# GpSimd makes every second low part of the MLP's hidden tiles, with new orders of the same matmuls and an earlier form of the last division

## The chip, the core and the metric

The kernel runs on one core of one Trainium2 chip. A core has five engines each with its own stream of instructions, which this kernel writes out by hand: TensorE (PE in the profile; PEld is its loading of weights), VectorE (DVE), ScalarE (ACT), GpSimd (POOL) and SyncE (SP), which here issues most of the transfers. They wait for one another through semaphores. Matmuls write to PSUM, of which the kernel uses eight banks of 128 partitions by 512 numbers in 32 bits; VectorE and ScalarE read the results there.

The metric is device time in microseconds, the median of three runs; less is better. Before the change it is 1000.59 us (1000.38 to 1000.65).

## The reference

An input x of 2048 rows by 448 columns is normalized, and two branches of the result are added to x: attention of 16 heads, 28 wide, that share one key and one value head, and a dense layer with ReLU, 1792 wide.

```python
xn = _layernorm(x, axis=-1)
return x + _A_ref(xn, A_wq, A_wk, A_wv, A_wo) + _B_ref(xn, B_w1, B_w2)

# _A_ref
scores = jnp.einsum("bhqd,bkd->bhqk", q, k) * (Dh ** -0.5)
p = _softmax(scores, axis=-1)
o = jnp.einsum("bhqk,bkd->bhqd", p, v)
... o @ wo
# _B_ref
h = jnp.maximum(jnp.einsum("bsd,df->bsf", x, w1), 0)
return jnp.einsum("bsf,fd->bsd", h, w2)
```

## The kernel before

**Precision.** Most products are made from a high part H in the format fp32r and a low part L, the rest: three passes, H by H, H by L and L by H, stand for one product. So every operand needs two instructions after it leaves PSUM: ScalarE copies the high part, and VectorE subtracts it from the bank to get the low part.

**The head** (to about 62 us). Rows are taken in four blocks of 512, four x tiles each. x arrives in `acc`, wq, wk and wv in `stg`. For each block the statistics are taken (L330, L331), x is normalized, transposed on TensorE (L371) and copied to `xt` in two parts (L373, L374). Four projections follow (`qkv_proj`, L429; L438 for the first three of block 0), each written out by `qkv_out`: ScalarE's and VectorE's `qs` (L415, L416), then a store to `qscr` in DRAM. Keys and values ride along in the spare columns of the four groups; `k_rows` (L400) picks the keys out of the `qs` of groups 0 and 1 with four matmuls, and `k_diff` makes differences of keys on GpSimd (`kD`, L411).

**The transfers' slots.** The transfers of SyncE and ScalarE share eight semaphores in turn, so an issue waits until the transfer eight places before it has landed.

**The MLP** (62 to about 384 us) has 28 tasks, seven parts of the weights by four blocks. A task has two up tiles (128 hidden columns by 512 rows: L707 `b<-xt,w`) and, two tasks later, four down tiles (128 rows by 448: L707 `b<-w,hH` and `b<-w,hL`). Each matmul uses 32 of the 128 rows of the array, and four row groups, numbered 0 to 3, work side by side. When an up tile is done, ScalarE makes hH with ReLU (L722) and VectorE hL (L724). When a down tile is done, ScalarE copies it to `y` (L731) and GpSimd adds that to `acc` (L732). GpSimd also splits the weights of the next part, in six steps over the tiles of one task in four (L306, L308).

**The maxima.** Softmax needs for each query the largest score. For each of 16 units (a block by a group of four heads) 64 matmuls of the high parts (L567) give scores whose maximum VectorE takes (L571): a single maximum. Or a pair: one matmul gives scores a, a second, with `kD`, gives the differences d, ScalarE makes max(d, 0) (`more`, L764), and VectorE adds it to a and takes the maximum (L575, with a short second instruction for the result): two maxima for one VectorE job. 445 of the 1024 maxima are made during the MLP.

**The attention** (384 to about 986 us). Scores (L609, three matmuls each), their exponentials on ScalarE (L620), p @ v (L827, four matmuls for one tile of 128 keys, 256 groups in all) and the output projection (L867). The sums of exponentials come with p @ v as a row of their own. The first 15 units are divided by way of DRAM; the last in `finish`: before the change a matmul with `dsel` spreads each sum over its head's rows, VectorE takes reciprocals of 128 columns (L894), GpSimd multiplies, and the last output projection (L904), its sum and its stores follow, the last tile in two halves on two queues.

**The order** is written out in two tables. In `ROWS` (MLP) a digit lets a row group issue its next matmul; a to d begin a tile, e to h join one, i to l make a single maximum, m to p and q to t the two halves of a pair, A to D early scores, each with the bank behind it; v takes a VectorE job that is owed. In `ORDER` (attention) `V` is a number of p @ v groups, `B` a burst (scores, maxima ahead by row group, maxima behind, banks), `O` and `f` matmuls of the output projection. The engines keep that order.

Of the kernel before, what the change touches and what calls it, by code (L numbers as in the profile page):

```python
# [8 lines left out]
F32 = mybir.dt.float32  # L9
# [22 lines left out]
    a3b4c5012012012012012d60123012301230123013o7i23f5s13e41g33vA0123012012p001vA2t2012012012p1012t7012vA  # L32
    0f6i21h51g431m0vA231q723123vA1a12310231023vA10231023f302l710g6l2102l01vA02h41023102vA31e52310231vA02
    310231023f10k7310k2310k0h3vA10310310vA31c7e6312031vB20312031203vAn2203r020h12vA0j43203203j5vA03e73vB
    03c3032b0302vB1302120d412vA031g1301230j5vA230f33201h02i21vA321i6321e432vA103f7203102l5vA01c2h30123e0
    123vB02310231023vA10g4l6102l512e3h21vA203b12031203vAg001320132i6h712i5312e231vA2031c303120vA31203102
    3f4i6213i0213e12vA1d502130213vA0f22301k63103vA10h3k01031g503vAj72032b40321vA3a621302130g11vA03120f53
    201p22e41t0201l7201h6201320f3vB32013e52130vAk0130g4l7102h11vA02310231i22vA312a031g602310vA23j5023020
    3j7vA2e33b20h41g003vA12302130213vA021302l510c71l1021vAh002130213i42vAf63i52132e213vB210d121031203vAf
    00313013vA0o41h70s31301c63f1023120132i5123vAa312301g230j02vA03f6203102l41vAe12l510210h321vA032f70321  # L40
    03vA21e63k00310l4g1102h21vA023102312i5vA312a031g303120vA32j40230j1230vA2j5e730h6g030vAf32301230123vA
    0123012d410c1vA3j5023f00231023vA1i6231m2231q3231vBa5230230vA2h003k60f430vAk331e1c7310231vA02h5102312
    03vA12301k2301k630h71k00vA31c3032f50321vA3e4213201h121vA031o203f7s60130k0130g5130213vB20132f303210vA
    321e7k6l0101g40l2102vAf102d51023e31vA23012301320vA13201l6201l0a7210g5vA1h32013203b22vA0321032103vAc6
    10d0210321302vA1320312e53o410l1s310h60g71302f0vA30123e212301vA23102l3102l1f502l41vA02101201g0vAl3012
    f6h7021vA230123i11231vAi5g231i423e023vA0b323012301vA230120l112e61vA20d5f7023103g3vA103210321i4321m0h
    2212q13vA1g53i6213e3213021vB302b4302130k1vA130c61e53201vA20h312031203vA120312i03132i7vA1d12f53213vAe
    4k213013c31302vA1h620j0230vA2f1302130k7130vA1k5301c23012vA30f3231i0213e12vA1h40210k73103vAf60k53103e
    31vA3k00130g11302vA103210231e2vA21l7021h30g43012vA30j523023e6j02vA30j12h20b72310vA32103210321vA031c5
    0d3b02031vA2031201321e732103vA2f2032103102vA310231e0k110d4j6g730vA230f323012301vA23e512l201g0l1012l6  # L50
    0vA12h702130213vA02130g413203vAj220h0b1203123vAe312301o6310s7310k2h5f4031013g1vB01230123012vA30j7232
    0b23k01e4vA31k60310g3h1102vA31023f5023i71vA23e212301l020vA1d62013021vA0321e13k4103c71032vB01320b0320
    13vA2i41321h221a3vB23103f620312vA031g003210p421e7t1210l52102h310g23vB123012301230vA23j102h0j50g630vA
    f33201321i432vA13i221h7i1213vA2e03j5203023vA02b4301g33012vA3e6123120312vA0j22d10k030f73g40vA13203120
    321vA0l52102d31g1031vA2i2312e431203vB12032103k0b50vA3c20132e11320vB1l620120h41203vA1g3031i03213vAe22
    3102l7012vA0f1l620120h51vA2i4132i013213vAf2c73123e312vA31023120312vA0n63k40r10h2f7k0vA031301g53012vB
    31023102d4i1vA32j032e7f3302vA130213021l20vA21p60g41t121vAe52h7102310231023vA1c003j22032f4d102130vB21
    302130c61vA30123e0j7203b220312vB0132013201l3vA2e41l702f1h0021vA30g213021302vA13e623102l5102l31c70l42
    10vA2h210231023vAf002310k53103g1vA10h7213i3213vAe22j4302f6302vA3102l510201d0vA2e731023103k31vA03o410
    3s210vA1e110g0d5f720312301vA230123012301o3h60b4s2301g5301230213e0213021302vA130o7130s2103vAc31e52012  # L60
    0f0021vAh40120312i1132vAi2132f5a73210vA32103c6103210vA23102f33i021p121t2vAg7e41l50212h601230vB123012
    301o03vA013s20h71k50303f6c1vB310231e323120vAl21201l520f7g40vA1l0201h12013vA210321032b20vA3120312e612
    0l5120h310k73f1vA0c0130213e212vB3012301203j5vA203b62031e123vA102l7102h201c4301vB230123e01230vA21302d
    510k7310g23j1203f4vA230123012h60vA12310g53102vA3n323r72i13f02e43120vBc23102301203120vAl712e5l11201g6
    0vAh4120310321vA032e2j33203j720h0f52vA03120132013vAa12130k4130k3f2301c7vA30120312e631vA201p520f1t421
    02h2103vA120312031203b3k00310h11vAc430123e71230vA213021302p210t51k001g1h4vA0213023023b6vB2302301g3l5
    vAi0121h72e41vA3201320n2302r1vA032j5032e632j00vB320f43c101320vA1h320123i5123vA1i223f7g6312vA31i02312
    e13120vA3120c4031vA20l5120h612e331vA2031203f1k2301c03012h40vB1321032103vA2j5032b203210h1vA213i6213e4
    2310vB3c7103201h0201vA23012i5312a6310k33vAf40k1310g2310vA2310123e71230vAj52h60b33021302vA130213e0213
    021h70o13j50s43f603g31032vA103210h221203vA1203f7o4031s513i1g613e3213021vB302f03021032vA10o51l7s11e2h  # L70
    3k4013vAk6013013013c1vB013201d720vA23b42031203vA10c33123e1123vA01230213021vA03o510l0s61h31g73vAf123i
    2132e4132vA013210p6210t0vA2f30210l5210h112301vBk2301c030f7230vA123e312l5021vAh402103k6103k11vA03c21e
    0320132vA012301230j5vA2303n3e7r60vAh2k1f003g41031230vB123013201p5vA20j1t620f220h012vA30123a313201vA3
    0c6130b12012vAl5012e2120vA12l70120h31203vA120312a03103c4vA03210h62j5023n2023r7vAe123f3031g0013vB2013
    201321023f4023vA10k5l710g31h0201vA320132e6j2320vAj5230g130h42vA0j73203f02031vA203123102vAd31023103j2
    2e43j5203f6c70vA3210l0201h120vA123e312301k20vA31031o5031s4vA031e7301c030f3230120d21vA20312a413201vA3
    20f7302130213012vA3i51g33i6123f4e02vA102l1120h712vA031g2031203j5vA230j6230b32h40vA13201321032vA1i132
    1m53f02q7vA1l6e31g40120vB120p1210t7210vA2d61e23103g310321032vAj50320n72h00r42vA30g6b1321032103210321
    vAa52310k43f2031k7031vAg10h312031203vA1230123012vA30k41d7013e113k0vA0f630g513021vB03210321a33120vA3n
    4203r020h1023j2023e6f723013vBk00130g31h502vA130213a221302vA103201k1301k4301c03vA2i6f33213e721vAh2201  # L80
    32013k11vA03k4f503130vA1h3k603103g21vA03210321032vA1h0i12132i413g7vAa613203f220312vA0p31201t1201vA2e
    0d41203f60231023vA10o5310s131a231k30f03vA01301g63012vBd101230123f42vA032103c710321l3021h6i5231e12vA3
# [85 lines left out]
def attention_plus_mlp(ctx: ExitStack, tc: tile.TileContext, x, wq, wk, wv, wo, w1, w2, out):  # L168
    nc = tc.nc
# [31 lines left out]
    for t in range(TPB):  # L201
        (nc.scalar if t % 2 else nc.sync).dma_start(acc[:, t, :], xv[:, t, :])
# [778 lines left out]
```

## Time and profile before

| | |
|---|---|
| median of three runs | 1000.59 us |
| the profiled execution | 1000.64 us |
| its span, first to last instruction | 998.9 us |
| matmuls (records in the trace) | 11686 |
| granted clock of TensorE, mean | 0.998 |
| transfers: moved, mean rate | 44.04 MB, 44 GB/s |

The profile is of one execution of the kernel. Its page gives the busy time of each engine, the same in 40 slices of the span (digits are tenths), the chain of work that ended last, and the costliest groups of instructions by line, with the mean time of one and the idle time before them with what ended it ("<-"). Further views list windows of time, waits, and the instructions in order of time. A busy TensorE is not one at its peak: its ends are modelled, so matmuls per microsecond say more. A wait counts only where the waiting engine holds up the end.

### The profile page before, as it was taken

Reading aid. Unit: us, or ns where it says so; the run is one execution under the profiler, and the core shown is the slowest. Engines: PE = TensorE matmul, PEld = TensorE weight load, DVE = VectorE, ACT = ScalarE, POOL = GpSimd, SP = SyncE. Lnnn points to the kernel's source line nnn. Section 1 sums busy time; section 2 is a strip of 40 time slices with the busy share of each in tenths; the row PEclk is TensorE's granted clock in tenths of the full one; section 3 lists DMA queues with packets and bytes.
Section 4 is the critical chain, followed back from the end, with each engine's and each line's share of the span. In section 5 each row is a group of like instructions: output and inputs, shape, how many; then the busy total and the mean of one; then the engine's idle time right before and its main releaser. Section 6 shows DMA issues by size and latency. Waiting matters only on the chain.

```text
span 998.9 us, 28752 instructions
## 1 busy us (share of the span) xinstructions
PE 990.0 (99%) x11686; PEld 632.0 (63%) x11686; DVE 716.8 (72%) x1301; ACT 696.2 (70%) x1340; POOL 250.4 (25%) x257
## 2 busy tenths in 40 slices
PE   9999999999999999999999999999999999999998
PEld 8779999999999995444444445444445433446444
DVE  7648999898888898988888876788776543743103
ACT  5533333434344446888899987899998799997993
POOL 4243475564646436010110110110110110110110
PEclk9999999999999999999999999999999999999999
DMA  7742201101010001101011001010111010000001
GB/s 241 259 138 84 62 23 33 42 14 42 14 52 3 14 2 46 33 14 46 13 34 43 26 23 57 16 46 23 24 35 42 31 34 24 13 13 29 23 13 37
DMA packets 31224, 44.04 MB, mean 44 GB/s; under 512 B 12228, under 2 KB 22788, under 8 KB 31092
## 3 DMA queue, kind: packets, MB, share of 16 engines
q1 hardware_dynamic: 24056, 32.72, 10.5%
q10 hardware_dynamic: 7036, 9.49, 3.1%
q8 instruction: 91, 1.49, 0.6%
q14 instruction: 41, 0.34, 0.1%
HBM read 29.62 MB, written 12.44 MB: 42 GB/s over the span
## 4 chain that ended last, share of the span: by engine, by line
PE 98%; DVE 1%; DMA 0%; ACT 0%; issue 0%; POOL 0%; DVEq 0%; ACTq 0%; POOLq 0%
PE o L827 25%; PE b L609 25%; PE b L707 24%; PE b L567 9%; PE b L867 4%; PE o L707 4%; PE b L429 3%; PE b L229 1%; PE b L438 1%; PE b L371 1%; PE o L567 0%; PE b L400 0%; DMA qscr<-qs 0%; PE b L904 0%; DVE rb L894 0%; PE o L429 0%
## 5 line engine op out<-in xcount | busy, mean ns | idle before, releaser
L571 DVE TENSOR_REDUCE nmx<-b 128x1 f32<-128x512 f32 x862 | 551.7, 684 | 158.6 <-PE b L567 110.6
L620 ACT ACTIVATE w<-b 128x512 f32<-128x512 f32 x1023 | 525.5, 616 | 74.1 <-PE b L609 69.5
L609 PE MATMUL b<-q,kHL 28*128 28x512 f32 (+1 forms) x3069 | 333.4, 425 | 0.2
L567 PE MATMUL b<-kHL,qhi 28*128 28x512 f32 x917 | 329.0, 448 | 1.1 <-ACT more L764 1.1
L609 PEld LDWEIGHTS b<-q,kHL 28*128 28x128 f32 (+1 forms) x3069 | 192.8, 183 | 186.3 <-DVE nmx L571 94.4
L707 PE MATMUL b<-xt,w 32*128 32x512 f32 x1974 | 290.7, 393 | 0.0
L707 PE MATMUL b<-w,hH 32*128 32x448 f32 x1616 | 276.0, 368 | 0.0
L827 PE MATMUL o<-w,vtile 128*32 128x512 f32 x2048 | 269.1, 607 | 0.2 <-ACT more L764 0.2
L707 PEld LDWEIGHTS b<-xt,w 32*128 32x128 f32 x1974 | 235.4, 183 | 3.3 <-DVE nmx L575 0.4
L707 PE MATMUL b<-w,hL 32*128 32x448 f32 x808 | 215.0, 364 | 0.0
L707 PEld LDWEIGHTS b<-w,hH 32*128 32x128 f32 x1616 | 206.6, 183 | 3.7 <-ACT y L731 0.5
L567 PEld LDWEIGHTS b<-kHL,qhi 28*128 28x128 f32 x917 | 150.5, 182 | 58.8 <-DVE nmx L571 25.6
L732 POOL TENSOR_TENSOR acc<-y,acc 128x448 f32<-128x448 f32 x112 | 128.0, 1154 | 125.6 <-ACT y L731 125.2
L851 POOL TENSOR_TENSOR on<-rb,oS 128x512 f32<-128x512 f32 x15 | 19.2, 1282 | 516.9 <-DMA rb<-rscr 314.1
L707 PEld LDWEIGHTS b<-w,hL 32*128 32x128 f32 x808 | 126.3, 183 | 0.2
L731 ACT ACTIVATE y<-b 128x448 f32<-128x448 f32 x101 | 54.7, 545 | 97.8 <-PE b L707 79.2
L827 PEld LDWEIGHTS o<-w,vtile 128*32 128x32 f32 x2048 | 43.2, 108 | 83.6 <-issue 78.9
L707 PE MATMUL o<-xt,w 32*128 32x512 f32 x378 | 95.2, 393 | 0.0
L707 PEld LDWEIGHTS o<-xt,w 32*128 32x128 f32 x378 | 66.9, 183 | 0.6 <-SPq L711 0.3
L764 ACT ACTIVATE more<-b 128x512 f32<-128x512 f32 x52 | 31.0, 598 | 38.8 <-PE b L567 27.8
L707 PE MATMUL o<-w,hH 32*128 32x448 f32 x176 | 50.5, 365 | 0.0
L722 ACT ACTIVATE hH<-b 128x512 fp32r<-128x512 f32 x47 | 28.0, 598 | 31.5 <-PE b L707 27.5
(112 smaller groups left out, 733.3 us busy)
## 6 DMA issues: line engine op xcount, KB each, us to landing
qscr<-qs SPq DMA_DIRECT2D x16, 512.0 KB
q<-qscr SPq DMA_DIRECT2D x12, 512.0 KB
rb<-rscr SPq DMA_DIRECT2D x60, 64.0 KB
out<-acc SPq DMA_DIRECT2D x15, 224.0 KB
acc<-in_A_x SPq DMA_DIRECT2D x14, 224.0 KB
qhi<-qscr SPq DMA_DIRECT2D x11, 256.0 KB
stg<-in_B_w ACTq DMA_DIRECT2D x5, 448.0 KB
q<-qscr ACTq DMA_DIRECT2D x4, 512.0 KB
```

The costliest lines, as they stand in the source:

```text
L429: nc.tensor.matmul(pq, w, xm, start=n == 0, stop=n == len(steps) - 1)
L567: nc.tensor.matmul(pm, qhi[u][rows, s * P : (s + 1) * P], k.rearrange("p k b q -> p (k b q)"), start=True, stop=True)
L571: nc.vector.tensor_reduce(dst, pm, axis=AX.X, op=ALU.max)
L609: nc.tensor.matmul(ps, keys, qst[u][rows, s, :], start=k == 0, stop=k == 2)
L620: nc.scalar.activation(p, ps, AF.Exp, scale=SCALE)
L707: mm = nc.tensor.matmul(o, w, m, start=self.left == self.n_mm - 1, stop=self.left == 0)
L722: nc.scalar.activation(hH, self.ps, AF.Relu)
L731: nc.scalar.activation(y, self.ps[:, 0:D], AF.Copy)
L732: nc.gpsimd.tensor_tensor(a, y, a, op=ALU.add)
L764: nc.scalar.activation(more, d[1], AF.Relu)
L827: nc.tensor.matmul(o_acc[u][RB * j : RB * (j + 1)], vtile[:, kb, :], ps[j], start=kb == 0, stop=kb == NKB - 1)
L867: nc.tensor.matmul(py[:, 0:D], om[:, i * P : (i + 1) * P], wm, start=n == 0, stop=n == len(steps) - 1)
```

## The change

It does six things.

- **Loads of the head.** Each of the first four x tiles comes in two halves of 224 columns, one from SyncE and one from ScalarE.
- **Key rows.** In blocks 1 and 2 `k_rows` and `k_diff` come after the fourth projection instead of before it; blocks 0 and 3 keep their place.
- **Low parts.** For the second up tile of each task ScalarE copies the ReLU twice, as hH and as `h` in full precision, and GpSimd subtracts. The buffers of `y` go from four to three.
- **ROWS** is a new table: 344 singles and 54 pairs instead of 319 and 63, with single maxima first; 443 VectorE jobs become 432.
- **ORDER** is a new table: 572 maxima instead of 579, 246 bursts instead of 247, the same scores and p @ v.
- **finish**: TensorE transposes the last unit, VectorE takes the four reciprocals of each row, GpSimd spreads them, TensorE transposes that back, VectorE multiplies; the last tile is summed and stored whole.

```diff
 ROWS = """
-    a3b4c5012012012012012d60123012301230123013o7i23f5s13e41g33vA0123012012p001vA2t2012012012p1012t7012vA
+    a3b4c5012012012012012d60123012301230123013k7i13f53g3e413vA2013201l22vA01l0201201l7vA201201201l1vA201
...
 ORDER = """
-    V2 R B6.0111..1265043162 B6.0.01.540316245 B4.11.001.063512641 B0.001..063 V2 B4.12.0.5421063 V1
+    V2 R B6.111.0.3204561235 B6.11.1.064312650 B0.0..1 V1 B7.000.113.4302165431062 V1 B4.02.1.1546320 V1
...
     for t in range(TPB):
-        (nc.scalar if t % 2 else nc.sync).dma_start(acc[:, t, :], xv[:, t, :])
+        for queue, cols in ((nc.sync, slice(0, D // 2)), (nc.scalar, slice(D // 2, D))):
+            queue.dma_start(acc[:, t, cols], xv[:, t, cols])
...
         qkv_out(b, 2, qkv_proj(b, 2))
-        k_rows(b, qs)
-        k_diff(b)
+        if last:
+            k_rows(b, qs)
+            k_diff(b)
...
         pq = qkv_proj(b, 3, middle=None if last else lambda: transposed(b + 1, xn))
         qkv_out(b, 3, pq)
+        if not last:
+            k_rows(b, qs)
+            k_diff(b)
...
                 nc.scalar.activation(hH, self.ps, AF.Relu)
+                if self.i == 1:
+                    h = dpool.tile([P, QB], F32, name="h")
+                    nc.scalar.activation(h, self.ps, AF.Relu)
+                    nc.gpsimd.tensor_tensor(hL, h, hH.bitcast(F32), op=ALU.subtract)
+                    return
                 owed.append(
...
-            y = dpool.tile([P, D], F32, name="y", bufs=4)
+            y = dpool.tile([P, D], F32, name="y", bufs=3)
...
-        for _ in range(3):
+        pt = [bank(i) for i in range(TPB)]
+        for _ in range(2):
             next(piece)
         for i, c in enumerate(cols):
-            pb = bank(i)
-            nc.tensor.matmul(pb[:, 0:P], dsel, oS[:, c], start=True, stop=True)
-            nc.vector.reciprocal(rb[:, c], pb[:, 0:P])
-            nc.gpsimd.tensor_tensor(on[:, c], oS[:, c], rb[:, c], op=ALU.mult)
-            next(piece)
+            nc.tensor.transpose(pt[i][:, 0:P], oS[:, c], ident)
+            den = pt[i][:, 0:P].rearrange("p (j c) -> p j c", j=HG)[:, :, DH : DH + 1]
+            nc.vector.reciprocal(r[:, i], den)
+            nc.gpsimd.tensor_scalar(rb[:, i], r[:, i].to_broadcast([P, HG, RB]), 1.0, 0.0, op0=ALU.mult, op1=ALU.add)
+            if i > 1:
+                next(piece)
+        for i, c in enumerate(cols):
+            pb = bank((TPB + i) % 6)
+            nc.tensor.transpose(pb[:, 0:P], rb[:, i].rearrange("p j c -> p (j c)"), ident)
+            nc.vector.tensor_tensor(on[:, c], pb[:, 0:P], oS[:, c], op=ALU.mult)
+            if i < 2:
+                next(piece)
...
-            halves = [slice(0, D)] if i + 1 < TPB else [slice(0, D // 2), slice(D // 2, D)]
-            for k, h in enumerate(halves):
-                nc.tensor.matmul(py[:, h], on[:, c], g3[:, h], start=True, stop=True)
-            for k, h in enumerate(halves):
-                nc.vector.tensor_tensor(acc[:, t, h], py[:, h], acc[:, t, h], op=ALU.add)
-                (nc.scalar if k else nc.sync).dma_start(out[t * P : (t + 1) * P, h], acc[:, t, h])
+            nc.tensor.matmul(py[:, 0:D], on[:, c], g3, start=True, stop=True)
+            nc.vector.tensor_tensor(acc[:, t, :], py[:, 0:D], acc[:, t, :], op=ALU.add)
+            nc.sync.dma_start(out[t * P : (t + 1) * P, :], acc[:, t, :])
```

How it moves instructions, at three places. A row is a line, an operation, what it writes and from what, its shape, a count, and the semaphores it waits for. The first place is SyncE at the start of the head, before:

```order
L202 DMA acc<-in_A_x 128x448 x2
L243 DMA stg<-in_A_wq 128x448 x3
L246 DMA stg<-in_A_wq 64x448
L247 DMA stg<-in_A_wq 64x448 [waits DMAHW0_49]
L245 DMA stg<-in_A_wk 128x3x28 [waits DMAHW1_49]
```

and in the change:

```order
L203 DMA acc<-in_A_x 128x224 x4
L244 DMA stg<-in_A_wq 128x448 [waits DMAHW0_49]
L244 DMA stg<-in_A_wq 128x448 [waits DMAHW1_49]
L244 DMA stg<-in_A_wq 128x448 [waits DMAHW2_49]
L247 DMA stg<-in_A_wq 64x448 [waits DMAHW3_49]
L248 DMA stg<-in_A_wq 64x448 [waits DMAHW4_49]
L246 DMA stg<-in_A_wk 128x3x28 [waits DMAHW5_49]
```

ScalarE issues as many x loads as SyncE, so the first wait for a slot (DMAHW) moves from wq's fifth load to its first, and every load behind it has one.

The second place is TensorE in block 2 of the head (`b_...` are banks, each number one use; L371 and L372 are transposes), before:

```order
L429 MATMUL b_596<-xt,w 128x512 x11
L429 MATMUL b_612<-xt,w 128x512 x11
L400 MATMUL b_628<-qs,ksel 128x512 x2
L400 MATMUL b_632<-qs,ksel 128x512 x2
L429 MATMUL b_645<-xt,w 128x512 x6
L371 MATMUL b_653<-ident,hH 128x128 x2
```

and in the change:

```order
L372 MATMUL b_668<-ident,hH 128x128 x2
L372 MATMUL b_668<-ident,hL 128x128 x2
L430 MATMUL b_639<-xt,w 128x512 x5
L401 MATMUL b_686<-qs,ksel 128x512 x2
L401 MATMUL b_690<-qs,ksel 128x512 x2
L430 MATMUL b_702<-xt,w 128x512 x11
```

The key rows (`qs,ksel`) stood between the third projection (b_612) and the fourth (b_645). Now they stand behind the fourth (b_639) and the transposes in its middle, and ahead of the next block's first (b_702).

The third place is ScalarE where the MLP begins, after the head's last `qs`; before:

```order
L415 ACTIVATE qs<-b_757 128x512 [waits DMAHW6_49,DVE_49,PE_49]
L764 ACTIVATE more<-b_838 128x512 [waits DMAHW3_49,DMAHW4_49,DMAHW2_49,DMAHW5_49,DVE_49,PE_49]
L764 ACTIVATE more<-b_865 128x512 [waits PE_49]
L764 ACTIVATE more<-o 128x512 [waits PE_49]
L764 ACTIVATE more<-o 128x512 [waits DVE_49,PE_49]
L722 ACTIVATE hH<-b_787 128x512 [waits PE_49]
```

and in the change:

```order
L416 ACTIVATE qs<-b_761 128x512 [waits DMAHW2_49,DVE_49,PE_49]
L727 ACTIVATE hH<-b_789 128x512 [waits PE_49,Pool_49]
L727 ACTIVATE hH<-b_791 128x512 [waits PE_49]
L730 ACTIVATE h<-b_791 128x512 [waits DMAHW1_49,DMAHW6_49,DMAHW0_49,DMAHW7_49,DVE_49,Pool_49]
L727 ACTIVATE hH<-b_810 128x512 [waits PE_49]
L730 ACTIVATE h<-b_810 128x512
```

Four copies for pairs are gone from the start; the first instruction that waits for transfers is now `h` of the first task, behind two copies hH.

More of the change, by code (lines that the diff above doesn't have):

```diff
@@ L37 @@
[L37 to L46, printed above, removed]
@@ L108 @@
+    Am11q6vAvAvA
 """
 ORDER = """
[L117 to L121 removed]
@@ L164 @@
+    B7...0164523 V1 O9,0 O2,1 B4...6452 f7 B4...3064 V1 B4...5213 V2 B4...0645 O9,2 B4...1306 V4
 """
@@ L921, in attention_plus_mlp @@
     g3 = wof[:, NHG - 1, :]
-    dsel = opool.tile([P, HG, RB], F32, name="dsel", bufs=1)
-    heads = ident.rearrange("p (j c) -> p j c", c=RB)[:, :, DH : DH + 1].to_broadcast([P, HG, RB])
-    nc.gpsimd.tensor_scalar(dsel, heads, 1.0, 0.0, op0=ALU.mult, op1=ALU.add)
-    dsel = dsel.rearrange("p j c -> p (j c)")
     steps, n_rows = None, 3
```

233 lines of the change are left out of this document (121 added, 112 removed).

## The prediction

> **What bounds the kernel now.** I read the page first, busy times, slices and chain.
>
> ```profile
> span 998.9 us, 28752 instructions
> PE 990.0 (99%) x11686; PEld 632.0 (63%) x11686; DVE 716.8 (72%) x1301; ACT 696.2 (70%) x1340; POOL 250.4 (25%) x257
> DVE  7648999898888898988888876788776543743103
> PE 98%; DVE 1%; DMA 0%; ACT 0%; issue 0%; POOL 0%; DVEq 0%; ACTq 0%; POOLq 0%
> ```
>
> TensorE is busy for 99% and is 98% of the chain of waits. A busy TensorE need not be at its peak, so the question is how many matmuls pass in a stretch. The view by windows tells it (length, then busy us and instructions of PE, PEld, DVE, ACT, POOL, then clock and DMA):
>
> ```profile
> 75.00:375.00 300.00, 300.00 (x5240) 287.92 (x5235) 266.45 (x499) 124.08 (x225) 154.48 (x137) 1.00 0.11 32
> 384.30:986.40 602.10, 601.90 (x5827) 273.10 (x5823) 389.93 (x663) 528.30 (x1031) 56.10 (x50) 1.00 0.10 29
> 62.20:87.20 25.00, 23.63 (x374) 20.93 (x377) 18.01 (x35) 7.35 (x13) 8.34 (x8) 1.00 0.16 54
> 87.20:112.20 25.00, 25.00 (x439) 23.49 (x435) 22.31 (x41) 9.58 (x18) 11.92 (x11) 1.00 0.31 100
> 67.20:72.20 5.00, 3.63 (x51) 2.75 (x52) 3.21 (x9) 2.28 (x4) 4.14 (x5) 1.00 0.00 0
> ```
>
> In the MLP (75 to 375) a matmul passes every 57 ns (300/5240), and the weight loads alone are busy for 288 of 300 us. VectorE has 266 us there, ScalarE 124, GpSimd 154: VectorE is full, yet TensorE does not wait for it. The exception is the MLP's first 25 us, with 374 matmuls against 439 in the next 25. In the attention part ScalarE has 528 of 602 us and VectorE 390; TensorE runs in short bursts there.
>
> The sum is made against the profiled execution, 1000.64 us (its span of 998.9 and 1.7 around it), which is 0.05 above the median of 1000.59.
>
> **The change part by part.**
>
> *The loads of the head.*
>
> ```profile
> 1.65 1.38 SPq L243 DMA_DIRECT2D stg<-in_A_wq  x3
> 4.49 0.48 SPq L247 DMA_DIRECT2D stg<-in_A_wq  x1
> 6.83 0.59 SPq L245 DMA_DIRECT2D stg<-in_A_wv  x1
> SPq L247 <- DMA acc<-in_A_x: 0.8, 1, 0.8
> 9.89 0.39 ACT L275 ACTIVATE w<-stg 128x56 fp32r<-128x56 f32 x2 [0.46 <-DMA stg<-in_A_wv]
> ```
>
> Two queues issue four x tiles and four loads of wq, and the ninth issue, at 4.49, has waited 0.8 us for the first x tile to land. In the change the first eight are the x halves, so wq's first load is the ninth: it moves from 1.65 to the landing of the first half, at most 4.49. Five wq and three wk loads at 0.48 to 0.59 each stand ahead of wv, so wv goes out at up to 9.0 instead of 6.83. ScalarE's copy at 9.89 already waits for wv (0.46 us), and behind it in ScalarE's queue stand the copies of x transposed that the first projection needs. Bounds: 0 (half a tile lands much sooner than a whole one, and wq then has the DMA engines to itself) and +2.2. I take +0.4, near the lower end, because the half tile should be there about a microsecond before the whole one and some slack remains before the projection. The later x tiles go out as much later; their statistics run behind the same delay.
>
> *The key rows after the fourth projection, blocks 1 and 2.*
>
> ```profile
> 32.51 0.19 PEld L400 LDWEIGHTS b<-qs,ksel 128*128 128x128 f32 x1 [0.43 <-DVE qs L416]
> 44.63 0.39 PE L400 MATMUL b<-qs,ksel 128*128 128x512 f32 x1
> 45.80 1.22 PE L400 MATMUL b<-qs,ksel 128*128 128x512 f32 x3 [0.77 <-ACT qs L415]
> 46.86 0.40 PE L429 MATMUL b<-xt,w 128*128 128x512 f32 x1
> 58.66 1.08 PE L400 MATMUL b<-qs,ksel 128*128 128x512 f32 x4
> 59.58 2.66 PE L429 MATMUL b<-xt,w 128*128 128x512 f32 x11
> ```
>
> Without a wait the four matmuls take 0.92 us (58.66 to 59.58, block 3, which keeps its place). In block 2 they take 2.23 (44.63 to 46.86): 1.3 us lost on qs. Block 1 loses about 0.3. In the change 11 matmuls and 16 transposes go first, so qs is long there: -1.6 (bounds -1.2, if the transposes then wait for the normalized x, and -1.6). What is late next is that x, ready some 0.5 us before its transposes by the same rows.
>
> *Single maxima first.*
>
> ```profile
> 67.69 1.09 ACT L764 ACTIVATE more<-b 128x512 f32<-128x512 f32 x2 [4.81 <-DMA qscr<-qs]
> 68.34 0.49 PE L567 MATMUL b<-kHL,qhi 28*128 28x512 f32 x1 [1.05 <-ACT more L764]
> ```
>
> The first pair's copy `more` lies in memory that the head's qs held, so it waits 4.81 us for their store to land, and TensorE stands. In the change the first maxima are single and need VectorE alone; the first instruction with that wait is the copy `h`, behind two finished up tiles, and the first up tile ends near 75 us. In 67.2 to 72.2 the row above has 51 matmuls where the later rate gives 88: 37 x 57 ns = 2.1 us. I take -2.1; bounds 0 (the reuse of banks waits for single reductions) and -3.7 (all 65 matmuls that the first 25 us lack).
>
> *GpSimd's hL, and the mix of maxima.*
>
> ```profile
> L571 DVE TENSOR_REDUCE nmx<-b 128x1 f32<-128x512 f32 x862 | 551.7, 684 | 158.6 <-PE b L567 110.6
> L724 DVE SCALAR_TENSOR_TENSOR hL<-b,hH 128x512 fp32r<-128x512 f32 x47 | 31.4, 681 | 1.8 <-ACT hH L722 1.5
> L764 ACT ACTIVATE more<-b 128x512 f32<-128x512 f32 x52 | 31.0, 598 | 38.8 <-PE b L567 27.8
> L575 DVE CUSTOM_DVE_ANT_0 more<-b,more 128x512 f32<-128x512 f32 x55 | 37.5, 683 | 9.8 <-ACT more L764 9.7
> L855 POOL TENSOR_TENSOR oL<-on,oH 128x512 fp32r<-128x512 f32 x15 | 19.3, 1284 | 1.3
> L732 POOL TENSOR_TENSOR acc<-y,acc 128x448 f32<-128x448 f32 x112 | 128.0, 1154 | 125.6 <-ACT y L731 125.2
> L308 POOL TENSOR_TENSOR w<-stg,w 128x640 fp32r<-128x640 f32 x21 | 33.0, 1572 | 1.3
> L306 POOL TENSOR_SCALAR w<-stg 128x640 fp32r<-128x640 f32 x21 | 15.3, 730 | 19.9 <-PE b L707 8.5 <-PE b L567 7.3 <-PE o L707 4.0
> ```
>
> VectorE loses 28 x 0.681 = 19.1 us; the tables give the MLP 344 singles and 54 pairs for 319 and 63, so it gains 25 x 0.684 - 9 x 0.683 = 11.0: net -8.1. ScalarE gains 28 - 9 copies of 0.598, 11.4 us, in a stage where it is busy for 124 of 300. GpSimd gains 28 x 1.284 = 36 us on 154. All of it is off TensorE's path, so I cost it at nothing; the weight loads' pace is the cover. The MLP does 452 maxima instead of 445: 7 x 57 ns = +0.4.
>
> A rule speaks against the move. The Trainium skill (GPSIMD Engine Reference, 4.1 Engine selection) gives elementwise work to VectorE and calls GpSimd about twice as slow with two inputs; 1284 against 681 ns agrees, and it costs only where GpSimd is waited for. Its section 1 (Specifications) adds that GpSimd shares its way into SBUF with VectorE, in contention with VectorE instructions of two SBUF inputs; by that the 36 us might come on top, 1032 at the very worst. The trace shows no such effect:
>
> ```profile
> 199.65 0.69 DVE L571 TENSOR_REDUCE nmx<-o 128x1 f32<-128x512 f32 x1
> 201.31 0.69 DVE L571 TENSOR_REDUCE nmx<-o 128x1 f32<-128x512 f32 x1 [0.37 <-PE o L567]
> 200.96 1.15 POOL L732 TENSOR_TENSOR acc<-y,acc 128x448 f32<-128x448 f32 x1 [1.30 <-ACT y L731]
> ```
>
> A reduction takes 0.69 us with GpSimd at work beside it (201.31) and without (199.65).
>
> *The attention's order.*
>
> ```profile
> 960.89 1.03 PE L609 MATMUL b<-q,kHL 28*128 28x512 f32 x12
> 961.85 1.06 PE L827 MATMUL o<-w,vtile 128*32 128x512 f32 x8
> 492.28 0.49 PE L609 MATMUL b<-q,kHL 28*128 28x512 f32 x2
> 493.64 1.07 PE L827 MATMUL o<-w,vtile 128*32 128x512 f32 x8
> ```
>
> A burst of four scores without a maximum takes 0.96 us to the next p @ v, one with three maxima 1.36, so a maximum costs about 0.13 here. The table has 572 for 579: -7 x 0.13 = -1.0. Else the two tables are alike: 143 bursts of four scores with three maxima (141 before), 45 with two (55), 35 with none (32), 229 groups of p @ v (230). Which banks a burst waits for I can't price; a tenth on the 0.2 us that 141 bursts may wait is 3 us, hence -1.0 +- 3.
>
> *The old division.*
>
> ```profile
> 989.17 3.39 DVE L894 RECIPROCAL rb<-b 128x128 f32<-128x128 f32 x4 [6.47 <-PE b L893]
> 991.90 3.31 PE L904 MATMUL b<-wo,on 128*128 128x448 f32 x10 [1.32 <-DVE rb L894]
> 995.97 0.36 ACTq L907 DMA_DIRECT2D out<-acc  x1
> ```
>
> Four reciprocals of 128 columns hold VectorE for 3.39 us and TensorE for 1.32. In the change a reciprocal has four columns, which takes most of the 3.39 away. Three steps come in for each piece: GpSimd spreads the result over 128 columns (between 0.15 us, a fifth of L306's 640 columns, and its whole 0.73), TensorE transposes it back, and VectorE, no longer GpSimd, makes the product (under L724's 0.68 for 512 columns). The four pieces run behind one another through four engines, so what counts is the way of the first piece and the pace of the slowest step. With 0.3 for the spreading, 0.3 for the product, 0.4 for the transpose and 0.2 for each of the hops between, all estimates from these rows, the last output projection starts 0.4 sooner than at 991.90; its last piece is then summed and stored whole on one queue instead of as two halves on two, 0.1 later: -0.3 (bounds -0.9, if the hops are short, and +0.8, if each step costs its upper bound).
>
> **Sum:** 0.4 - 1.6 - 2.1 + 0.4 - 1.0 - 0.3 = -4.2, so 996.4 us.
>
> **The rivals.** *The stall only changes its name:* banks wait for VectorE's singles at the MLP's start, and the head's loads come 1.2 late. Then +1.2 - 1.6 + 0 + 0.4 - 1.0 - 0.3 = -1.3, 999.3. For it: VectorE needs 0.6 us for each of the first 12 maxima. Against it: VectorE was busy for only 3.21 us of that stretch's 5, so there is room.
>
> *GpSimd becomes the bound (slower).* A task of the MLP lasts 322/28 = 11.5 us. In the task that splits a weight part GpSimd has 4 x 1.154 + 1.284 + 3 x (0.730 + 1.572) = 12.8 us, 1.3 too many; if ScalarE's y, with three buffers instead of four, then waits for GpSimd and holds the banks, six such tasks cost 6 x 1.3 = 7.8: 1004.2. It decides once GpSimd lies more than three down tiles behind, some 5 us. Against it: the next task leaves 5 us to catch up.
>
> *VectorE's relief counts in full:* if TensorE did wait for VectorE in the MLP, 8.1 us more, 988.3. Against it: 57 ns per matmul at 89% of VectorE.
>
> **How the numbers follow.** Forecast 0.66, own range 994 to 998.5; the renamed stall 0.17; GpSimd 0.11; relief 0.05; the shared way into SBUF 0.01. A measurement of this kernel tells 0.2%, 2 us, from no change: faster is below 998.6 (forecast, relief and a little of the renamed stall, 0.73), same 0.15, slower 0.12. The range, 993.5 to 1000.5, holds forecast and renamed stall with the attention's unknown.
>
> **What would show it.** Right: no wait of TensorE on qs in blocks 1 and 2, no ScalarE wait on qscr ahead of the maxima, some 410 matmuls in the MLP's first 25 us, 57 ns per matmul after that with VectorE less busy, bursts as before. Wrong: wv awaited for over 1.5 us at the first copies; y's ScalarE copy waiting for GpSimd; bursts with three maxima above 1.4 us; more than 11 us from the last p @ v to the end.

## The result, and the profile after the change

The changed kernel takes 1012.16 us (median of four runs, 1009.13 to 1015.26) against 1000.62 (1000.38 to 1000.95) for the kernel before beside it: ratio 1.011, 95% interval 1.009 to 1.013. It is 1.1% slower, where 996.4 was forecast, and far outside the range. The profiled execution took 1011.45 us. Its page, first lines and chain of waits:

```profile
span 1009.7 us, 28803 instructions
PE 994.6 (99%) x11684; PEld 636.0 (63%) x11684; DVE 712.6 (71%) x1276; ACT 702.6 (70%) x1359; POOL 284.5 (28%) x284
PE 95%; DVE 2%; POOL 1%; DMA 1%; ACT 0%; issue 0%; ACTq 0%; DVEq 0%
```

TensorE's share of the chain falls from 98% to 95%. VectorE's doubles to 2%, GpSimd and transfers now have 1% each: some 30 us that have to be found in place. I cut the span at six points that both traces have: starts of TensorE's matmuls, in us. The last column is the best version of the experiments.

| stretch | before | changed | best |
|---|---|---|---|
| head, to the first matmul of the MLP | 62.2 | 61.2 | 60.5 |
| its first 840 matmuls without the maxima | 56.1 | 54.1 | 54.6 |
| the rest of the MLP, to its last matmul | 263.4 | 273.0 | 263.8 |
| from there to the 17th group of p @ v | 46.7 | 52.4 | 44.9 |
| from there to the last p @ v | 559.1 | 559.0 | 559.8 |
| end | 11.4 | 10.0 | 10.0 |
| span | 998.9 | 1009.7 | 993.6 |

Up to 115 us the change has gained 3.0 us, near the 3.3 that the forecast had for the head and the first maxima. It loses 9.6 in the rest of the MLP and 5.7 in the passage to the attention. The view by windows of the changed kernel (length, then busy us and instructions of PE, PEld, DVE, ACT, POOL, then clock and DMA) has the MLP's first 25 us, its body, and eight us of it:

```profile
61.20:86.20 25.00, 25.00 (x408) 23.80 (x408) 20.04 (x33) 6.96 (x13) 12.95 (x12) 1.00 0.24 84
75.00:375.00 300.00, 295.43 (x5066) 280.44 (x5061) 260.08 (x471) 127.55 (x238) 188.09 (x163) 0.99 0.11 32
182.00:184.00 2.00, 0.67 (x13) 0.29 (x5) 1.86 (x5) 1.09 (x2) 2.00 (x3) 1.00 0.36 109
184.00:186.00 2.00, 1.83 (x24) 1.51 (x27) 2.00 (x5) 0.00 (x0) 2.00 (x2) 0.88 0.08 25
186.00:188.00 2.00, 2.00 (x25) 2.00 (x22) 1.90 (x4) 0.54 (x1) 0.42 (x2) 0.50 0.05 9
188.00:190.00 2.00, 2.00 (x34) 1.94 (x30) 1.03 (x2) 0.16 (x1) 0.87 (x1) 0.76 0.01 1
```

5066 matmuls pass in 300 us where 5240 did. The lack is not spread: from 182 to 190 there are 96 matmuls where the pace of 57 ns gives 140, first because TensorE stands, then because its granted clock is halved (0.50 from 186 to 188). The instructions in order of time show what it stands for, here in the first place of this kind (VectorE, GpSimd, and TensorE where it goes on):

```profile
130.82 2.26 POOL L742 TENSOR_TENSOR acc<-y,acc 128x448 f32<-128x448 f32 x2
131.76 0.22 DVE L586 TENSOR_REDUCE nm<-nmx 128x16 f32<-128x64 f32 x1
132.01 1.10 DVE L587 CAST nm<-nm 128x16 fp32r<-128x16 f32 x1
133.03 1.56 POOL L309 TENSOR_TENSOR w<-stg,w 128x640 fp32r<-128x640 f32 x1
133.15 1.48 DVE L588 TENSOR_TENSOR nm<-nm,nm 128x16 fp32r<-128x16 f32 x1
134.54 1.28 POOL L731 TENSOR_TENSOR hL<-h,hH 128x512 fp32r<-128x512 f32 x1
134.66 0.21 DVE L590 STREAM_TRANSPOSE rows<-nm 128x32 f32<-128x32 f32 x1
134.79 0.65 DVE L576 TENSOR_REDUCE nmx<-b 128x1 f32<-128x512 f32 x1
135.50 0.49 PE L572 MATMUL b<-kHL,qhi 28*128 28x512 f32 x1 [1.62 <-DVE nmx L576]
```

These are the finals of a unit (`max_final`): the maxima's last reduction (L586), then a copy in fp32r (L587) and a subtraction (L588) that split 16 numbers per partition into high and low part. Both are tiny, 0.17 us where nothing else happens. Here the copy takes 1.10 and ends at 133.11, 0.03 after GpSimd's sum (130.82 + 2.26 = 133.08); the subtraction takes 1.48 and ends at 134.63, 0.04 after GpSimd's 134.59. The reduction before and the transpose behind them run beside GpSimd at their usual 0.22 and 0.21. Behind the finals in VectorE's queue stand the singles, whose banks TensorE needs: it starts no matmul between 133.51 and 135.50. The view of the tile has all sixteen finals (minimum, median and maximum ns):

```profile
L586 DVE TENSOR_REDUCE nm<-nmx x16: 219/220/222, 131.8 to 947.8; 128x16 f32<-128x64 f32 x16
L587 DVE CAST nm<-nm x16: 174/175/2604, 132.0 to 948.0; 128x16 fp32r<-128x16 f32 x16
L588 DVE TENSOR_TENSOR nm<-nm,nm x16: 174/174/1477, 133.1 to 948.5; 128x16 fp32r<-128x16 f32 x16
```

Of the twelve such copies and subtractions up to 392 us eight are long (copies at 132, 181, 252, 283 and 391, subtractions at 133, 182 and 332), and each ends within 0.05 us of the end of a GpSimd instruction. Before the change two were: the copies at 142.46 (0.37) and 287.98 (0.48). The same view of the kernel before:

```profile
L582 DVE CAST nm<-nm x16: 174/174/479, 142.5 to 935.9; 128x16 fp32r<-128x16 f32 x16
L583 DVE TENSOR_TENSOR nm<-nm,nm x16: 174/174/176, 142.9 to 936.2; 128x16 fp32r<-128x16 f32 x16
```

The worst, 2604 ns, is at the passage to the attention, again in order of time:

```profile
389.25 3.35 POOL L742 TENSOR_TENSOR acc<-y,acc 128x448 f32<-128x448 f32 x3 [1.06 <-ACT y L741]
391.55 2.60 DVE L587 CAST nm<-nm 128x16 fp32r<-128x16 f32 x1
392.53 1.60 POOL L931 MEMSET wo<- 128x1792 f32 x1
394.54 1.84 DVE L576 TENSOR_REDUCE nmx<-b 128x1 f32<-128x512 f32 x3
394.64 1.78 ACTq L456 DMA_DIRECT2D nscr<-rows  x4
395.24 0.95 PE L614 MATMUL b<-q,kHL 28*128 28x512 f32 x5 [2.53 <-DVE nmx L576]
396.48 3.05 ACT L625 ACTIVATE w<-b 128x512 f32<-128x512 f32 x6 [5.94 <-DMA nscr<-rows]
```

Two things meet. The copy waits out the last sum and the memset behind it (392.53 + 1.60 = 394.13). And ScalarE, which in the MLP issues transfers too, has the four stores of these finals (`ACTq`, L456) ahead of its first exponentials: it stands for 5.94 us. In the kernel before the sixth unit ended behind the MLP's table, and SyncE issued these stores (L457 at 389.75) while ScalarE ran exponentials from 385.34 on.

A third, smaller thing is in the view of waits (engine, what waited for what, us in total, times, longest), from 62 to 400 us:

```profile
ACT y L741 <- POOL acc L742: 5.7, 5, 2.1
```

The copy y waits for GpSimd, whose sums still hold the three buffers.

### The profile page after: what moved, and what is told of

It is laid out like the page before. It is cut to its first block, busy times and chain, and to the rows that moved or that the text cites. A ratio compares the mean times of both kernels' runs of the same rounds, so it can differ in the third digit from the quotient of the medians.

```text
span 1009.7 us, 28803 instructions
## 1 busy us (share of the span) xinstructions
PE 994.6 (99%) x11684; PEld 636.0 (63%) x11684; DVE 712.6 (71%) x1276; ACT 702.6 (70%) x1359; POOL 284.5 (28%) x284
## 4 chain that ended last, share of the span: by engine, by line
PE 95%; DVE 2%; POOL 1%; DMA 1%; ACT 0%; issue 0%; ACTq 0%; DVEq 0%
PE o L837 25%; PE b L614 25%; PE b L712 23%; PE b L572 9%; PE b L877 4%; PE o L712 3%; PE b L430 3%; DVE nmx L576 1%; PE b L439 1%; PE b L372 1%; DVE nm L587 0%; DMA acc<-in_A_x 0%; DVE nm L588 0%; PE o L572 0%; PE b L401 0%; POOL acc L742 0%
## 5 line engine op out<-in xcount | busy, mean ns | idle before, releaser
L576 DVE TENSOR_REDUCE nmx<-b 128x1 f32<-128x512 f32 x879 | 561.2, 684 | 173.7 <-PE b L572 131.7
L572 PE MATMUL b<-kHL,qhi 28*128 28x512 f32 x927 | 335.2, 454 | 4.0 <-DVE nmx L576 3.0
L614 PEld LDWEIGHTS b<-q,kHL 28*128 28x128 f32 (+1 forms) x3072 | 197.8, 184 | 183.4 <-DVE nmx L576 102.2
L712 PE MATMUL b<-xt,w 32*128 32x512 f32 x2058 | 299.9, 394 | 0.1
L712 PE MATMUL b<-w,hH 32*128 32x448 f32 x1552 | 279.8, 369 | 1.5 <-ACT y L741 1.2
L712 PEld LDWEIGHTS b<-xt,w 32*128 32x128 f32 x2058 | 243.9, 183 | 2.9 <-ACT y L741 0.5
L712 PE MATMUL o<-xt,w 32*128 32x512 f32 x294 | 76.1, 400 | 0.0
L712 PE MATMUL o<-w,hH 32*128 32x448 f32 x240 | 69.3, 367 | 0.0
L712 PEld LDWEIGHTS o<-xt,w 32*128 32x128 f32 x294 | 52.8, 186 | 0.7 <-DVE nmx L576 0.3
L774 ACT ACTIVATE more<-b 128x512 f32<-128x512 f32 x43 | 25.8, 599 | 36.0 <-PE b L572 20.1
```

What stands on the lines that cost most here:

```text
L572: nc.tensor.matmul(pm, qhi[u][rows, s * P : (s + 1) * P], k.rearrange("p k b q -> p (k b q)"), start=True, stop=True)
L576: nc.vector.tensor_reduce(dst, pm, axis=AX.X, op=ALU.max)
L614: nc.tensor.matmul(ps, keys, qst[u][rows, s, :], start=k == 0, stop=k == 2)
L712: mm = nc.tensor.matmul(o, w, m, start=self.left == self.n_mm - 1, stop=self.left == 0)
L774: nc.scalar.activation(more, d[1], AF.Relu)
```

## The experiments

Four theories: **A**, the finals' copy and subtraction stand still beside GpSimd; **B**, GpSimd's backlog holds y, h and the banks; **C**, the stores that ScalarE issues at the end of the MLP hold its exponentials; **D**, the new order's first bursts are slow by their own banks. Every kernel computes the whole reference. Each was measured beside the kernel before, whose medians there are 1001.09, 1000.88 and 1001.24; the ratios are to these.

**Finals of reductions only** (changed kernel).

```diff
-        nm = small.tile([P, HG, 1, TPB], F32, name="nm")
+        nm = small.tile([P, HG, TPB, 2], F32R, name="nm")
...
-        nc.vector.tensor_reduce(nm, nmx.pop(u), axis=AX.X, op=ALU.max, negate=True)
-        nc.vector.tensor_copy(t[:, :, 0:1], nm)
-        nc.vector.tensor_tensor(t[:, :, 1:2], nm, t[:, :, 0:1].bitcast(F32), op=ALU.subtract)
+        m = nmx.pop(u)
+        nc.vector.tensor_reduce(nm[:, :, :, 0].bitcast(F32), m, axis=AX.X, op=ALU.max, negate=True)
+        nc.vector.tensor_reduce(nm[:, :, :, 1], m, axis=AX.X, op=ALU.max)
+        nc.vector.tensor_reduce(t[:, :, 0], m, axis=AX.X, op=ALU.max, negate=True)
...
+            nc.vector.tensor_reduce(t[:, :, 1], nm.bitcast(F32), axis=AX.X, op=ALU.add)
```

The first two reductions write the negative maximum in full precision and, beside it, the maximum in fp32r; the third writes the negative high part; the fourth adds the pair, which gives the low part. No copy and no subtraction is left.

> The changed kernel, but the split of a unit's final maxima into high and low part is made by four VectorE reductions instead of one reduction, a copy (L587) and a subtraction of two SBUF operands (L588). Theory A, VectorE's copy and subtraction stand still until the GpSimd instruction beside them ends: all of these stalls go (about 2.8 us lost at 132-135, 3.4 at 181-190, 1 at 252 and 283, 0.9 at 332, some 5 at 391-405 with the halved clock behind it), so 998 to 1001. Theory B, GpSimd's backlog holds ScalarE's y (three buffers) and the banks: the finals' form does not matter, 1009 to 1013.

Measured: 1000.08 us (998.69 to 1003.05), ratio to before 0.9989 (0.9979 to 0.9998): 12.1 less than the changed kernel. The tile's view of this kernel, two of the three reductions that replace copy and subtraction:

```profile
L588 DVE TENSOR_REDUCE nm<-nmx x16: 207/209/214, 131.5 to 939.6; 128x16 fp32r<-128x64 f32 x16
L591 DVE TENSOR_REDUCE nm<-nm x16: 174/178/181, 131.7 to 939.9; 128x16 fp32r<-128x32 f32 x16
```

None of the sixteen is long. Theory A holds; with GpSimd's work and both tables untouched, B cannot explain 12.1.

**The same finals in the kernel before.**

> The kernel before with the same four reductions in the finals. Its two met copies cost 0.2 and 0.3 us of VectorE, against 0.3 us more work in each of 16 finals. Theory A and B: within 1 us of before, 999.6 to 1001.6.

Measured: 1000.98 (998.55 to 1002.91), ratio 1.000 (0.9989 to 1.0011). There the copies hardly met GpSimd, and nothing is to be gained.

**A GpSimd instruction put beside the finals** (kernel before, nine finals of the attention; its result is not used).

```diff
...
+        if u > 6:
+            beside = small.tile([P, 8, HG * TPB * 4], F32, name="beside", bufs=1)
+            wide = m.rearrange("p (o j) s h -> p o (j s h)", o=1).to_broadcast([P, 8, HG * TPB * 4])
+            nc.gpsimd.tensor_tensor(beside, wide, wide, op=ALU.subtract)
...
```

> The kernel before, with one GpSimd subtraction of 512 columns added beside each of the last nine finals, where GpSimd is idle otherwise; it is released by the same maxima as the final's first reduction, and nothing uses its result. Theory A: the copy takes about 1.0 to 1.3 us instead of 0.17 in each of the nine, and ends with GpSimd's instruction; the first reduction and the transpose keep 0.22 and 0.21. If the long copies of the changed kernel came from something else in the MLP: 0.17 in all nine. In time 0 to +6, since VectorE has room there.

Measured: 1002.95 (1001.65 to 1004.19), ratio 1.0015 (1.0005 to 1.0024). One of the nine in order of time:

```profile
597.42 0.22 DVE L586 TENSOR_REDUCE nm<-nmx 128x16 f32<-128x64 f32 x1
597.47 1.04 POOL L585 TENSOR_TENSOR beside<-nmx 128x512 f32<-128x512 f32 x1 [4.98 <-DVE nmx L571]
597.68 0.86 DVE L587 CAST nm<-nm 128x16 fp32r<-128x16 f32 x1
598.57 0.17 DVE L588 TENSOR_TENSOR nm<-nm,nm 128x16 fp32r<-128x16 f32 x1
598.78 0.21 DVE L590 STREAM_TRANSPOSE rows<-nm 128x32 f32<-128x32 f32 x1
```

The copy takes 0.86 instead of 0.17 and ends (598.54) with GpSimd (598.51); the median over all sixteen finals is now 860 ns. It is a little shorter than expected (1.0 to 1.3), since GpSimd starts before the copy. The subtraction, behind GpSimd's end, has its 0.17. So the stall is made at will, outside the MLP. The Trainium skill (SBUF — State Buffer, Who interferes with whom) says the same: VectorE's copies and casts in their two-port mode, and its instructions with two SBUF inputs (where GpSimd reads SBUF too), share a pair of ports with GpSimd and block for a whole instruction, while reductions never contend on trn2. The runs agree for the copy, the subtraction and the reductions; that the copy runs in that mode no run here shows.

**Four buffers of y** (changed kernel; h has one buffer instead of two, for the room).

```diff
-                    h = dpool.tile([P, QB], F32, name="h")
+                    h = dpool.tile([P, QB], F32, name="h", bufs=1)
...
-            y = dpool.tile([P, D], F32, name="y", bufs=3)
+            y = dpool.tile([P, D], F32, name="y", bufs=4)
```

> The changed kernel with four buffers of y instead of three (and one of h instead of two, for the room). Theory A: only the waits of y for GpSimd at 313 and 318 go, about -2, so 1009 to 1011. Theory B: the MLP gets back most of its loss, 1002 to 1006.

Measured: 1010.84 (1010.44 to 1016.42), ratio 1.0106 (1.0086 to 1.0126): at most a small part, as A expects; against the changed kernel the ranges overlap, though y's wait for GpSimd's sums falls from 5.7 to 1.1 us.

**The left-over transfers on SyncE, with the finals of reductions.**

```diff
-            (soon if first else later).append(lambda: nc.scalar.dma_start(dst, src))
+            (soon if first else later).append(lambda: (nc.scalar if while_mlp else nc.sync).dma_start(dst, src))
...
+    while_mlp = False
     for issue in soon + later:
         issue()
-    while_mlp = False
```

> The changed kernel with the four reductions in the finals, and the transfers that are left over when the MLP's table ends issued by SyncE instead of ScalarE. Theory C, the table ends a unit's maxima inside the MLP, so that ScalarE issues the four stores of its finals and stands in front of the first exponentials until VectorE has the rows (3.4 us in the run with the reductions, 5.9 in the changed kernel), after which TensorE's clock is halved: about 3 less than the run with the reductions alone, 996 to 998. Rival D, the attention's first bursts are slow by their own banks: 999.5 to 1001.

Measured: 997.74 (996.93 to 997.94), ratio 0.9964 (0.9951 to 0.9976): 2.3 less than with the reductions alone, and the ranges do not touch. ScalarE at the passage, with the reductions alone:

```profile
383.86 0.63 ACT L777 ACTIVATE more<-b 128x512 f32<-128x512 f32 x1
386.11 1.73 ACTq L456 DMA_DIRECT2D nscr<-rows  x4
387.89 3.04 ACT L628 ACTIVATE w<-b 128x512 f32<-128x512 f32 x6 [3.39 <-DMA nscr<-rows]
```

and with SyncE as well:

```profile
382.96 0.63 ACT L777 ACTIVATE more<-b 128x512 f32<-128x512 f32 x1
385.55 5.99 ACT L628 ACTIVATE w<-b 128x512 f32<-128x512 f32 x12 [1.97 <-PE b L572]
```

Twelve exponentials run through where six did, and none waits for a store. C holds, D does not.

**The left-over transfers on SyncE alone** (changed kernel).

> The changed kernel with only the left-over transfers moved from ScalarE to SyncE; its finals keep copy and subtraction. Theory A and C together: the stalls in the MLP stay (+7 to +8), the copy at the MLP's end still stands 2.6 us beside GpSimd's sum and memset, but the first exponentials no longer wait for it: 1005 to 1009. If the copy's stall alone decides there (no part for ScalarE's wait): 1011 to 1013.

Measured: 1012.50 (1008.27 to 1012.73), ratio 1.0096 (1.0077 to 1.0116): a miss. It is no different from the changed kernel, and lies in the range that was given for the copy's stall deciding alone. In its profiled execution, the shortest of the five, the first exponentials come at 392.48 instead of 396.48, but the copy still takes 2.60, and TensorE stands for the singles behind it, as before (2.52 us until 395.20). What ScalarE's stores cost was thus seen in the times only once the finals run.

**All three: reductions, SyncE, four buffers of y.**

> The same with four buffers of y and one of h. The run with the reductions alone lost some 3 us at 311 to 313, where y waited for GpSimd's sum: without it 994 to 996.5. If one buffer of h makes ScalarE wait for GpSimd instead: the same as with three buffers, 996 to 998.

Measured: 995.67 (995.34 to 997.24), ratio 0.9950 (0.9936 to 0.9964). It beats both kernels. Against the run before it the ranges overlap (995.34 to 997.24, 996.93 to 997.94), and part of the 2.1 is TensorE's clock: three of these five executions had a mean of 1.000, one of the other five. At 1.000 the two differ by 1.3 to 1.6, at 0.998 by 0.1 to 0.8. The waits of y for GpSimd's sums in it, same view as above:

```profile
ACT y L744 <- POOL acc L745: 1.1, 2, 0.7
```

**GpSimd's part alone** (kernel before with its old tables, the second low part by way of h, three buffers of y; VectorE's places for these low parts stay empty), and the same with the reductions.

```diff
                 nc.scalar.activation(hH, self.ps, AF.Relu)
+                if self.i == 1:
+                    h = dpool.tile([P, QB], F32, name="h")
+                    nc.scalar.activation(h, self.ps, AF.Relu)
+                    nc.gpsimd.tensor_tensor(hL, h, hH.bitcast(F32), op=ALU.subtract)
+                    owed.append(lambda: None)
+                    return
```

> The kernel before with one part of the change alone: the second low part by way of h on GpSimd and three buffers of y, the old tables (the VectorE jobs of these low parts are left empty). Theory A: the finals meet a busier GpSimd, a loss of 1 to 3 us at each of some four of six finals, 1003 to 1010. Theory B (backlog): 1004 to 1010 as well. If VectorE's 19 us less counted: below 999.

> The same with the four reductions in the finals. Theory A: the loss goes, 999.5 to 1002. Theory B: it stays, 1004 to 1010.

Measured: 1003.52 (1000.74 to 1005.45), ratio 1.0021 (1.0012 to 1.0030), and 1002.46 (1000.41 to 1004.26), ratio 1.0015 (1.0007 to 1.0024). I expected more of A here. With the old table only three copies meet GpSimd (0.67, 0.73 and 0.50 us) and no subtraction, so the reductions bring 1.1 at most, and the intervals overlap; 1002.46 lies in neither forecast's range. That trace is of the one execution at a mean clock of 1.000 (1000.74), where the kernel before took 998.44 to 999.26 in three executions of the comparisons: a loss of 1.5 to 2.3. In both kernels y waits once for 4.3 us in the MLP; whether that is the loss was not tried. VectorE's 19 us less bring nothing with the old table.

**The second low part back on VectorE.** First at once, ahead of all VectorE jobs that are owed (changed kernel):

```diff
-                    h = dpool.tile([P, QB], F32, name="h")
-                    nc.scalar.activation(h, self.ps, AF.Relu)
-                    nc.gpsimd.tensor_tensor(hL, h, hH.bitcast(F32), op=ALU.subtract)
+                    nc.vector.scalar_tensor_tensor(
+                        hL, self.ps, 0.0, hH.bitcast(F32), op0=ALU.max, op1=ALU.subtract
+                    )
```

> The changed kernel with the second low part back on VectorE behind its hH: GpSimd has 28 x 1.28 = 36 us less in the MLP, VectorE 19 more. Theory A: GpSimd is busy for about half of the MLP instead of 0.63, the finals still meet it at times and the memset at 392 still does: 1001 to 1008. Theory B: no backlog, 996 to 1000.

Measured: 1044.66 (1041.85 to 1045.93), ratio 1.0429 (1.0410 to 1.0448), which no theory had. The view of waits, 62 to 400 us:

```profile
DVE hL L729 <- ACT hH L727: 25.9, 26, 2.4
```

VectorE stands at its place for ScalarE's hH, 26 times a microsecond, with the singles behind it: the experiment measured the place as much as the load. So again, behind the second VectorE job that follows, with the reductions, SyncE's transfers and four buffers of y:

> The changed kernel with reductions, SyncE's transfers and four buffers of y, and the second low part on VectorE, behind the second VectorE job that follows it, without h. If VectorE has room in the MLP (the prediction's cover, the weight loads' pace): 994 to 998, as with GpSimd. If VectorE is full with the 25 singles more that the new table gives it: 1003 to 1020; then what GpSimd takes off it is needed.

Measured: 1012.09 (1011.05 to 1012.63), ratio 1.0104 (1.0089 to 1.0119), 16.4 more than the best version. The windows of this kernel,

```profile
75.00:375.00 300.00, 293.38 (x4943) 271.12 (x4942) 262.20 (x493) 112.03 (x204) 147.52 (x130) 1.00 0.11 32
```

and of the best version:

```profile
75.00:375.00 300.00, 299.92 (x5234) 287.80 (x5234) 259.13 (x485) 132.04 (x246) 195.08 (x170) 1.00 0.10 32
```

At the best version's pace VectorE would need 262.2 x 5234 / 4943 = 278 of 300 us with the low parts, and TensorE waits for the low parts, in the view of waits (62 to 400 us) of the kernel with VectorE's low parts:

```profile
PEld b L572 <- DVE hL L734: 11.5, 17, 1.8
PE b L572 <- DVE hL L734: 5.4, 10, 1.4
```

Without them 259 do, and a matmul passes every 57 ns. Place and load are still not apart here: VectorE was busy for 266 of 300 us before the change, and TensorE did not wait. A table made for low parts on VectorE was not tried.

**The head's and the end's parts alone** (kernel before with the halved loads, the later key rows and the old division, word for word as in the change).

> The kernel before with three parts of the change alone: the halved x loads, the key rows of blocks 1 and 2 behind the fourth projection, the old division. By the prediction's terms (+0.4, -1.6, -0.3): 999.4. By the stages of the runs so far (+0.4, -1.5, -1.4): 998.3.

Measured: 999.79 (997.30 to 1003.87), ratio 0.9983 (0.9970 to 0.9996), 1.45 below the kernel before of the same comparison (1001.24), as the terms had it together, but not stage by stage. In its profile head and end are 2.9 shorter (60.7 and 10.0), but the passage to the attention (48.3) and the attention behind it (560.3) are 2.8 longer than in the kernel before. The windows of the passage, of the kernel before and of this one, show a difference in the clock (0.89 and 0.68):

```profile
384.00:400.00 16.00, 15.91 (x125) 7.62 (x125) 13.36 (x27) 10.41 (x21) 8.64 (x6) 0.89 0.30 71
384.00:400.00 16.00, 16.00 (x111) 8.23 (x111) 12.17 (x24) 10.21 (x21) 6.50 (x4) 0.68 0.30 70
```

If it was 0.50 where it fell, as in the windows of the changed kernel, it was halved for some 3.5 us and some 10 us of the 16; by this estimate the difference can cost up to 3.4 us of TensorE's work. The two executions of the eleven with a mean clock of 1.000 took 997.30 and 997.43, below both expected times. What sets the clock back there was not tried.

## Why the prediction was wrong, by its steps

**The step that failed** is "All of it is off TensorE's path, so I cost it at nothing; the weight loads' pace is the cover". The sentence that guarded it, "The trace shows no such effect", rested on a row that cannot show one: a reduction from a bank (0.69 us with GpSimd beside it and without). The effect belongs to instructions that copy within SBUF or take two SBUF operands, and the trace of before had them, 16 of each: copies (`CAST`) of 0.17, but of 0.37 and 0.48 where they met GpSimd's sums. Taking copy and subtraction out of the finals gives back 12.1 us. In the profiled execution VectorE itself loses 9.2 us in eight such instructions (their durations less 0.17 each); TensorE pays by standing and then by its clock.

I had this as a rival with a chance of 0.01, and priced it by GpSimd's total (36 us on top) instead of by the few VectorE instructions that can be hit and what is queued behind them. Why the new table is hit in eight of twelve places and the old in two, or three with GpSimd's part: GpSimd is busy for 188 of 300 us instead of 154, which is too little for it; the rest is where the finals fall beside GpSimd's work. That is argued from the traces, not tried.

**A step that was missing:** the attention's order was priced by its bursts, and the stretch from the 17th group on came out within the forecast (559.0 against 559.1; forecast -1.0 +- 3, though 7 x 0.13 is 0.9). Its beginning was not looked at. There the MLP's table now ends with the sixth unit's finals, and the stores move from SyncE to ScalarE, ahead of the exponentials: 2.3 us by the medians once the finals run. The order of ScalarE's instructions at the end of the MLP shows it before anything runs.

**The rival of GpSimd as the bound** named a true wait, y's three buffers, at the wrong size: at most the 2.1 us between the last two versions (997.74 and 995.67), not 7.8.

**The other terms.** Loads: the first projection starts at 11.84 instead of 11.35 (+0.5, forecast +0.4; 11.3 to 12.1 in the nine profiles with the halves, 11.2 to 11.4 in the five without). With the key rows the MLP starts 1.0 earlier (forecast 1.2), and no matmul of L401 waits. Single maxima first: 2.0 us in the first 840 matmuls (forecast 2.1), and 408 matmuls in 25 us (forecast some 410); the wait on qscr is gone, and no other took its place. Old division: the end is 1.4 shorter, forecast 0.3 and bounded at 0.9. The rows of its steps, from the changed kernel's trace in order of time:

```profile
1001.08 0.83 DVE L906 RECIPROCAL rf<-b 128x4 f32<-128x4 f32 x4 [5.30 <-PE b L904]
1001.35 1.09 POOL L907 TENSOR_SCALAR rb<-rf 128x128 f32<-128x128 f32 x4 [22.99 <-DVE rf L906]
1002.14 1.12 DVE L913 TENSOR_TENSOR on<-b,oS 128x128 f32<-128x128 f32 x4 [0.23 <-PE b L912]
1002.86 3.17 PE L921 MATMUL b<-wo,on 128*128 128x448 f32 x8
```

Spreading and product take 0.27 and 0.28 a piece, as estimated, and the first piece is through in 1.8 us (1001.08 to 1002.86). The terms of the forecast add up to 1.8, and 2.0 with a reciprocal of 0.2; from where the reciprocals stood before, 1.7 us behind the last p @ v, they give a last projection 0.7 sooner, so the 0.4 was a wrong sum. Another 0.3 is that the reciprocals now start 1.4 us behind the last p @ v, which no term had. In all the last projection starts 3.2 us behind it instead of 4.4.

**"TensorE does not wait for VectorE"** held for the table of before. The new table spends what GpSimd takes off: with 25 singles more and the low parts on VectorE the kernel is 16.4 slower. With this table, and the low parts where they were put, the move to GpSimd is worth that much.

**The sum** of the forecast (-4.2) is near that of the change without its three collisions (-5.2, 995.67 against 1000.88), but in part by luck. At a mean clock of 1.000 the kernel before took 998.44 to 999.26 and the best version 995.34 to 995.67: 2.8 to 3.9 between them. And not every stage came as its term: the end gave 1.4 instead of 0.3, and the attention's order gave 1.1 (forecast 1.0) as 1.8 at the passage, where the kernel before has its clock set back (0.89 above) and the best version does not, less 0.7 behind it.

## What to carry to other kernels

An engine that gets more work off the critical path can still stop another one: before moving work to GpSimd, list VectorE's instructions that copy within SBUF or read two SBUF operands, however small, look at their longest duration and not their mean, and ask what is queued behind them. A row clears such an effect only if its operands are of the kind that the effect needs. And where a new order moves the end of a unit across a stage's edge, look which queue its transfers now stand in.

## What the runs showed of the hardware

Between two GpSimd instructions that follow each other at once, a waiting VectorE copy got its turn in one place and not in another. The copy at 132.01 ended at 133.11, with the sum that ended at 133.08, though the next GpSimd instruction had started at 133.03. The one at 391.55 let a sum end at 392.60 and then stood out the memset that had started at 392.53, to 394.13. What decides was not tried.

A pause of TensorE with 1.41 us without a matmul (182.31 to 184.07 from start to start) was followed by a clock of 0.50 from 186 to 188 in the windows above, and the one at 392 to 395 by 0.50 from 398 to 404; the longer pause at 133.51 (1.62 us without a matmul) was followed by no drop. In the run with SyncE's transfers alone it was the other way round: 0.50 from 138 to 140 behind the first of these pauses, 1.00 from 184 to 192 behind the second. And in the kernel with the head's and the end's parts alone the clock fell to 0.68 over 16 us for all of which TensorE counts as busy. The Trainium skill (TensorE: Matmul & The Clock Gate, What's actually happening) puts the halving behind an idle window of about 3.4 us; here 1.41 us were followed by it once.
